# Prologue of a fused RWKV attention and soft-MoE kernel: identity copies on ScalarE, buffer clears on VectorE

## The chip, the cores and the metric

The kernel runs on one core of one Trainium2 chip. The core has five engines that the text calls by their names in the profile: PE (TensorE, matmul; PEld is its weight load), DVE (VectorE), ACT (ScalarE), POOL (GpSimd) and SP (SyncE, which issues loads). The metric is device time of one execution in microseconds (us); lower is better. Times inside an execution count from the start of the profile's span.

## The reference

The first stage is a linear attention with a decaying state, for 4 batches, 8 heads, 768 steps and head size 48. The second is a soft mixture of experts over the 3072 rows that the first one gives, with 32 slots in 8 experts.

```python
for t in range(S):                                # attention, state is D x D per batch and head
    cur = einsum('bhd,bhe->bhde', u * k[t], v[t])
    y[t] = einsum('bhd,bhde->bhe', r[t], state + cur)
    state = w * state + einsum('bhd,bhe->bhde', k[t], v[t])
...
logits = x @ phi                                  # x: 3072 x 384, phi: 384 x 32
slot_input = softmax(logits, axis=0).T @ x
slot_out = relu(slot_input[e] @ w1[e]) @ w2[e]    # per expert, 4 slots each
out = softmax(logits, axis=1) @ slot_out
```

## The kernel before

The attention is computed in chunks of 128 steps. Powers of `w` are taken up into `k` and `r` beforehand: `k` is multiplied by `w^-j` and `r` by `w^j`, with `j` the place in the chunk. The tables of these powers are `tabs` (for the short tiles, one third of the steps of a batch) and `tabl` (for the long tiles, two thirds). The attention of a chunk is then a masked matrix product, plus a product with the state.

The body of the kernel is a list of small tasks. Their order is written out by hand in the string `ORDER`; a task is put on the engine that stands behind its colon or on the first one that it allows. Each engine runs its tasks in that order. Names begin with a letter for the kind and end with the number of the tile or unit. The ones that the prediction touches are:

- `Lk0`, `Lr0`, `Lv0` and so on: loads from SP (L195).
- `Sk0`, `Sr0`, `Sk1a` and so on: the product of `k` or `r` with its table into a bf16 buffer of the tile `mix` (L423), on DVE for tile 0 and for `Sk1b`, else on POOL.
- `Tk0`, `Tr0`: transposes of such a buffer on PE (L432), with `turn` or `turnl` as the moving operand, which also sorts the steps. `Ek0`, `Er0`: the eviction (L356).
- `VC0`: the cast of `v` to bf16 on POOL (L414).
- `TB0a` and its sisters: exponentials that fill `tabl` (L393) on ACT, from arguments that DVE puts into `xT_all` (L281).
- `CB`: `consts_b`, a clear of `Mb`, two reductions of `ident_f` (L339 to L341) on DVE, and two copies on ACT (L342, L344).
- `CA` and `CU`: the transposed `w` and `u` are copied to `wuT` (DVE, L313) and multiplied into `ucol` (POOL, L316).
- `F0_3`, `F1y_9` and so on: fill matmuls that keep PE busy (L849); their results are not used.

Before these tasks stands the prologue (L209 to L304 and L330), written in plain order. POOL makes two identities, `ident` in bf16 and `ident_f` in f32, and an upper triangle `up_b`, by clears and `affine_select`. Three permuted copies of `ident` follow: `idp` (L255, DVE), which PE multiplies with `up_b` and `ident` to get the mask and the permutation `permT`; `turn` (L260, DVE, two halves); and `turnl` (L263, POOL). After the first two products PE runs thirteen warming matmuls on zeros (`keep_warm(13)`, L219). POOL clears the padding columns of the six `k` and `r` buffers in `mix` (L271), which each hold 48 columns of data in every 64, and then `ucol`, `wT`, `selp`, `nm`, `acc`, `Lc`, `uns` and one column of `x` (L296 to L331).

On DVE the prologue computes the exponents of the table (`expos_a`, L244, and `expos_b`, L247 to L249) and copies `permT` out of PSUM (L283). Then ACT takes the logarithm of `w` (L284), DVE multiplies it with the exponents into `AT_all` (L281, two halves), and ACT takes the exponentials into `tabs` (L288, L289). ACT starts with the issue of the load of `w` (L211) and a load of its function table (L212).

Of the kernel before, what the change touches and what calls it, by code (L numbers as in the profile page):

```python
# [81 lines left out]
def kernel(  # L82
# [13 lines left out]
    B, H, S, D = r.shape  # L96
# [9 lines left out]
    nQ = H // 2  # L106
    NP = B * nQ
    R = 8
    J = C // R
# [16 lines left out]
    def O(ins):  # L126
        return tc.keep_in_program_order(ins)

    pe, dve, act, pool, sp = nc.tensor, nc.vector, nc.scalar, nc.gpsimd, nc.sync
# [55 lines left out]
    Y_t = [Yb[:, j, :] for j in range(2)]  # L185
# [41 lines left out]
    ident = cst.tile([128, 128], bf, name="ident")  # L227
# [24 lines left out]
    expos_b(e17, float(JH // nQ))  # L252

    idp_t = cst.tile([128, C], bf, name="idp")
    O(dve.tensor_copy(idp_t[:].rearrange("p (j r) -> p j r", j=J), ident[:].rearrange("p (r j) -> p j r", r=R)))  # L255
    idp = idp_t[:]

    turn = cst.tile([128, 128], bf, name="turn")
    for c in range(CC):
        O(dve.tensor_copy(turn[:, 64 * c:64 * c + 64].rearrange("p (q s r) -> p q s r", q=nQ, s=2),  # L260
                          ident[:, 64 * c:64 * c + 64].rearrange("p (r s q) -> p q s r", q=nQ, s=2)))
    turnl = cst.tile([128, 128], bf, name="turnl")
    O(pool.tensor_copy(turnl[:].rearrange("p (c q r) -> p c q r", q=nQ, r=R), ident[:].rearrange("p (c r q) -> p c q r", q=nQ, r=R)))  # L263
    mask = cst.tile([128, C], f32, name="mask")
    permT = cst.tile([128, C], bf, name="permT")
# [2 lines left out]
    keep_warm(13)  # L268
    expos_a(nQ * (R - 1))
    for t in ks_t:  # L270
        O(pool.memset(t.rearrange("p (x s) -> p x s", s=64)[:, :, D:64], 0.0))  # L271

    av = AT_all[:].rearrange("p a b -> p (a b)").bitcast(f32)
    AVW = P2 * (JH + 1)
# [3 lines left out]
    def argv_part(dst, ex):  # L278
        n = ex.shape[1]
        for e in range(2):  # L280
            O(dve.tensor_mul(dst[:, e], lnw.rearrange("p (e d) -> p e d", e=2)[:, e, None, :].to_broadcast([128, n, D]),  # L281
                             ex[:, :, None].to_broadcast([128, n, D])))
    O(dve.tensor_copy(permT[:], Y_t[1][:, 0:128]))  # L283
    O(act.activation(out=lnw, in_=w_f, func=AF.Ln))  # L284
    argv_part(argv, e17[:, 0:JH + 1])
    expos_b(e17l, float(J // nQ))
# [49 lines left out]
                               phi_f[:, q, :].rearrange("p (g j s) -> p g j s", g=2, s=Spe)))  # L336

    def consts_b():
        O(dve.memset(Mb[:], 0.0))  # L339
        O(dve.tensor_reduce(out=sel[:], in_=ident_f[:].rearrange("p (b c) -> p c b", b=B), axis=AX.X, op=ALU.add))  # L340
        O(dve.tensor_reduce(out=blk[:], in_=ident_f[:].rearrange("p (b c) -> p b c", b=B), axis=AX.X, op=ALU.add))  # L341
        O(act.copy(selp[:].rearrange("p (j x) -> p j x", x=32)[:, :, 0:2 * Spe],  # L342
                   sel[:].rearrange("p (j x) -> p j x", j=EG)))
        O(act.copy(rep4[:], sel[:, None, :].to_broadcast([128, B, ES])))  # L344
# [40 lines left out]
    for j, f in enumerate((zeros_b, consts_p)):  # L385
        add(f"CB{j}", "POOL", (lambda f: lambda t: f())(f), deps=["LP"] if j else [])
    add("CB", "DVE", lambda t: consts_b())

    for h, av_, x in (("a", argl, slice(0, JH + 1)), ("b", argm, slice(JH, J + 1))):
# [578 lines left out]
```

## Time and profile before

| what | value |
|---|---|
| median of 3 runs | 124.03 us (124.11, 122.61, 124.03) |
| profiled execution, its own time | 124.79 us |
| span from first to last instruction | 123.0 us |
| busy share of the span: PE, DVE, ACT, POOL | 84%, 78%, 69%, 52% |
| mean granted TensorE clock | 0.945 |
| HBM traffic over the span | 359 GB/s |

A row of the timeline gives start, duration, engine, line, operation, output and input tiles with their shapes, and how many instructions were merged into it. In square brackets it has the time that the engine stood idle before, and what ended that. The page's second part divides the span into 40 slices with the busy share of each engine in tenths; the first six slices cover the prologue and the start of the task list. The granted clock is given per stretch as a share of full speed.

### The profile page before, as it was taken

What the parts mean: (1) busy time and instruction counts of PE and PEld (TensorE: products, weight loads), DVE (VectorE), ACT (ScalarE), POOL (GpSimd) and SP (SyncE); (2) the same over time, 40 slices, a digit from 0 to 9 for tenths busy, and PEclk for the clock granted to TensorE, in tenths of its full rate; (3) what the DMA queues carried; (4) which work ended last, traced back from release to release, by engine and by line L of the source; (5) the groups of instructions that cost most, each with busy time, mean ns of one, the idle gap of its engine ahead of it and who ended that gap; (6) DMA issues with size and microseconds to landing.
All of it is one profiled execution on the core that took longest, in us unless ns stands there. A gap on an engine that the chain in (4) does not pass through costs nothing.

```text
span 123.0 us, 4044 instructions
## 1 busy us (share of the span) xinstructions
PE 103.5 (84%) x1723; PEld 77.0 (63%) x1729; DVE 95.5 (78%) x176; ACT 84.6 (69%) x135; POOL 63.5 (52%) x85
## 2 busy tenths in 40 slices
PE   4959939999999999999999989999889979797000
PEld 1317526888888887888687877877454738573000
DVE  6989973789999999899999999999787710189000
ACT  4057569498999899999989999978744350187000
POOL 7930888899999999999999510310000000000000
PEclk9999985599999999999999999999999999999955
DMA  2999999999999899999999999999999980039994
GB/s 34 319 402 412 378 401 395 379 368 402 372 403 353 163 218 215 212 221 212 214 213 212 219 220 209 214 219 214 211 220 216 204 154 11 0 127 417 412 416 164
DMA packets 10697, 31.81 MB, mean 259 GB/s; under 512 B 1336, under 2 KB 4664, under 8 KB 10680
## 3 DMA queue, kind: packets, MB, share of 16 engines
q0 software_dynamic: 2592, 12.58, 50.4%
q1 hardware_dynamic: 7944, 18.93, 40.8%
q8 instruction: 13, 0.21, 0.7%
q10 hardware_dynamic: 144, 0.05, 0.4%
q14 instruction: 4, 0.03, 0.1%
HBM read 39.42 MB, written 4.72 MB: 359 GB/s over the span
## 4 chain that ended last, share of the span: by engine, by line
PE 51%; DVE 24%; ACT 11%; issue 4%; DMA 2%; DVEq 0%; ACTq 0%
PE T L432 9%; PE Ab L502 5%; PE T L591 4%; ACT mix L356 4%; DVE AT_all L507 4%; PE Yb L568 3%; DVE mix L935 3%; PE Yb L563 3%; PE Yb L903 3%; DVE mix L423 3%; PE T L477 2%; DVE AT_all L281 2%; PE Yb L574 2%; PE Mb L903 2%; DMA LexpT<-in_w_dram 2%
## 5 line engine op out<-in xcount | busy, mean ns | idle before, releaser
L507 DVE TENSOR_TENSOR AT_all<-Ab,mask 128x1024 bf16<-128x1024 f32 x24 | 29.1, 1214 | 1.1 <-PE Ab L502 1.1
L423 POOL TENSOR_TENSOR mix<-raw,tabl 128x768 bf16<-128x768 f32 x15 | 27.8, 1869 | 0.5 <-ACT tabl L393 0.3
L356 ACT COPY mix<-T 128x1024 bf16<-128x1024 bf16 x18 | 17.7, 1017 | 2.2 <-PE T L432 2.1
L432 PEld LDWEIGHTS <-mix 128*128 128x128 bf16 x192 | 12.1, 101 | 5.5 <-issue 2.7
L551 DVE TENSOR_TENSOR dv<-vn,Mb 128x768 bf16<-128x768 bf16 x12 | 11.3, 943 | 2.9 <-ACT wT L323 2.9
L423 POOL TENSOR_TENSOR mix<-raw,tabs 128x768 bf16<-128x768 f32 x6 | 10.9, 1825 | 0.9 <-PE T L432 0.9
L356 ACT COPY vT_all<-T 96x1024 bf16<-96x1024 bf16 x10 | 10.1, 1014 | 1.5 <-PE T L432 1.1
L356 ACT CAST x<-Yb 128x768 bf16<-128x768 f32 x12 | 9.7, 811 | 1.2 <-PE Yb L574 0.6
L502 PE MATMUL Ab<-mix 64*128 64x128 bf16 x192 | 9.8, 222 | 0.9 <-ACT mix L356 0.6
L432 PE MATMUL T<-turnl,mix 128*128 128x128 bf16 x128 | 10.1, 231 | 0.1
L356 ACT COPY xT_all<-T 128x768 bf16<-128x768 bf16 (+1 forms) x12 | 9.1, 787 | 1.4 <-PE T L591 1.3
L356 ACT COPY vn<-T 128x768 bf16<-128x768 bf16 x12 | 9.6, 811 | 0.0
L414 POOL CAST vj<-raw 128x768 bf16<-128x768 f32 x10 | 8.2, 829 | 0.9 <-DMA raw<-in_v_dram 0.9
L356 ACT COPY kn<-T 128x768 bf16<-128x768 bf16 (+1 forms) x11 | 7.8, 714 | 1.2 <-PE T L477 1.1
L448 DVE TENSOR_TENSOR pr<-T,mix 128x1024 bf16<-128x1024 bf16 x12 | 8.1, 680 | 0.1
L502 PEld LDWEIGHTS <-mix 64*128 64x128 bf16 x192 | 5.8, 95 | 3.1 <-issue 0.8
L568 PEld LDWEIGHTS <-AT_all 128*128 128x128 bf16 x192 | 6.6, 96 | 1.6
L219 PE MATMUL T<-LexpT 128*128 128x512 bf16 x15 | 6.0, 567 | 1.5 <-DVE LexpT L215 1.5
L432 PEld LDWEIGHTS <-vj 128*96 128x96 bf16 x96 | 6.7, 129 | 0.5 <-issue 0.2
L477 PE MATMUL T<-ident,mix 128*128 128x128 bf16 x80 | 6.9, 229 | 0.0
L535 DVE TENSOR_TENSOR Z<-Mb,wT 128x384 bf16<-128x384 f32 x12 | 6.6, 550 | 0.3 <-PE Mb L528 0.3
L568 PE MATMUL Yb<-vn,AT_all 128*128 128x48 bf16 x192 | 6.8, 183 | 0.0
(188 smaller groups left out, 256.1 us busy)
## 6 DMA issues: line engine op xcount, KB each, us to landing
raw<-in_moe_w_dram POOLq DMA_DIRECT2D x13, 768.0 KB, 13.3
raw<-in_k_dram SPq DMA_DIRECT2D x4, 768.0 KB, 11.4
raw<-in_r_dram SPq DMA_DIRECT2D x4, 768.0 KB, 11.7
raw<-in_v_dram SPq DMA_DIRECT2D x4, 768.0 KB, 12.1
out_dram<-mix SPq DMA_DIRECT2D x3, 768.0 KB, 4.9
raw<-in_k_dram SPq DMA_DIRECT2D x4, 384.0 KB, 9.7
raw<-in_r_dram SPq DMA_DIRECT2D x4, 384.0 KB, 9.9
raw<-in_v_dram SPq DMA_DIRECT2D x4, 384.0 KB, 10.0
```

The source lines that it names most:

```text
L356: O(act.copy(dst, src))
L414: O(act.copy(o, i_) if t.eng == "ACT" else pool.tensor_copy(o, i_))
L423: O(eng.tensor_mul(src.inst.rearrange("p (j e s) -> p e j s", j=JH, e=2)[:, :, :, 0:D], rv(), tab))
L432: O(pe.transpose(Tb.inst[0:P, jj * 128:(jj + 1) * 128], sv[:, jj, :], (turn, turnl)[lg][:]))
L448: O(dve.tensor_mul(cv(pb), tv(), cv(kT)))
L477: O(pe.transpose(Tb.inst[:, x * 128:(x + 1) * 128], kT.inst[:, x, :], ident[:]))
L502: O(pe.matmul(Abf.inst[:, e, x * C:(x + 1) * C], kT.inst[s, g * nQ + x, :], rT.inst[s, g * nQ + x, :]))
L507: O(dve.tensor_mul(AT.inst[:], Abf.inst[:].rearrange("p e (g t) -> p e g t", g=nQ), mask[:, None, None, :].to_broadcast([128, 2, nQ, C])))
L535: O(dve.tensor_mul(Smid.inst[:], Mf.inst[:, 0:SW].rearrange("p (q d) -> p q d", q=nQ)[:, :, None, :].to_broadcast([128, nQ, 2, D]), wT[:, ...
L551: O(dve.tensor_mul(dvb.inst[:].rearrange("p g e d -> p (g e) d"), vn.inst[:].rearrange("p g e d -> p (g e) d"), Mf.inst[:, 448:448 + 2 * P ...
L568: O(pe.matmul(y[:, x // nQ, q * P2 + e * D:q * P2 + (e + 1) * D], a[x // nQ].inst[:, e, q, :], vn.inst[:, x, e, :], start=False, stop=(c = ...
L903: O(pe.matmul(SO[h][32 * x:32 * x + 32, :], hT[g][:, y, 32 * x:32 * x + 32], w2_of(g * EG + x)[:, y, h * Dm // 2:(h + 1) * Dm // 2], start ...
```

## The change

Three edits in the prologue. The copies of the identity into `idp` and `turn` go from DVE to ACT, at the same place in the program; on ACT they follow the table load and precede the logarithm. The six clears of the `k` and `r` buffers go from POOL to DVE, again at the same place, which is after `expos_a` and ahead of the products into `AT_all`. And DVE's copy of `permT` out of PSUM moves from the prologue to the head of `consts_b`, that is, behind `Sk1b` in DVE's order. The copy of `turnl` and POOL's other clears stay where they are.

```diff
     idp_t = cst.tile([128, C], bf, name="idp")
-    O(dve.tensor_copy(idp_t[:].rearrange("p (j r) -> p j r", j=J), ident[:].rearrange("p (r j) -> p j r", r=R)))
+    O(act.copy(idp_t[:].rearrange("p (j r) -> p j r", j=J), ident[:].rearrange("p (r j) -> p j r", r=R)))
...
     for c in range(CC):
-        O(dve.tensor_copy(turn[:, 64 * c:64 * c + 64].rearrange("p (q s r) -> p q s r", q=nQ, s=2),
-                          ident[:, 64 * c:64 * c + 64].rearrange("p (r s q) -> p q s r", q=nQ, s=2)))
+        O(act.copy(turn[:, 64 * c:64 * c + 64].rearrange("p (q s r) -> p q s r", q=nQ, s=2),
+                   ident[:, 64 * c:64 * c + 64].rearrange("p (r s q) -> p q s r", q=nQ, s=2)))
...
     for t in ks_t:
-        O(pool.memset(t.rearrange("p (x s) -> p x s", s=64)[:, :, D:64], 0.0))
+        O(dve.memset(t.rearrange("p (x s) -> p x s", s=64)[:, :, D:64], 0.0))
...
-    O(dve.tensor_copy(permT[:], Y_t[1][:, 0:128]))
     O(act.activation(out=lnw, in_=w_f, func=AF.Ln))
...
     def consts_b():
+        O(dve.tensor_copy(permT[:], Y_t[1][:, 0:128]))
         O(dve.memset(Mb[:], 0.0))
```

## The prediction

> **What bounds the kernel now.** I read the page first (VectorE 78% busy, TensorE 84%, so no single engine is full), then the chain of waits, then the timeline of the first 24 us engine by engine, because every edited line runs there. All times below are microseconds from the start of the span. The chain of waits, with its start and length in the first two columns:
>
> ```profile
> 0.73 2.58 DMA LexpT<-in_w_dram
> 3.34 0.29 ACT LexpT L284
> 3.65 3.00 DVE AT_all L281 x2
> 6.66 0.94 ACT tabs L288 x2
> ...
> 13.52 2.14 DVE mix L423
> ...
> 16.50 0.22 ACT selp L342
> ...
> 21.59 1.06 PE T L432 x8
> ```
>
> The reader is to see that the two products of L281 take 3.00 us on the chain, although the same instruction form takes 0.59 us each when it fills `xT_all` at 10.1. The timeline of 4.6 to 5.4 us shows why they are slow (start, duration):
>
> ```profile
> 2.68 3.88 DVE L260 COPY turn<-ident 128x64 bf16<-128x64 bf16 x1
> 2.93 3.64 DVE L244 TENSOR_SCALAR pl<-pi 128x17 int32<-128x17 int32 x1
> 3.28 3.29 DVE L283 CAST permT<-Yb 128x128 bf16<-128x128 f32 x1
> 3.65 2.92 DVE L281 TENSOR_TENSOR AT_all<-LexpT,e 128x432 f32<-128x432 f32 x2
> ```
>
> Five instructions start at their normal pace and all end between 6.56 and 6.58. The second `turn` copy is the oldest of them; its twin took 0.31. GpSimd's timeline gives what stands beside them:
>
> ```profile
> 2.65 0.28 POOL L263 COPY turnl<-ident 128x128 bf16<-128x128 bf16 x1
> 2.88 1.57 POOL L271 MEMSET mix<- 128x256 bf16 x6
> ...
> 6.35 0.16 POOL L328 MEMSET x<- 128x6 bf16 x2
> 7.44 0.82 POOL L414 CAST vj<-raw 128x768 bf16<-128x768 f32 x1 [0.93 <-DMA raw<-in_v_dram]
> ```
>
> GpSimd runs clears with no gap from 2.88 to 6.51, and VectorE's five ends follow 0.05 after. I read this as one SBUF-to-SBUF copy that cannot write while GpSimd writes, and everything behind it retiring in order. TensorE's timeline and the windows (length, busy time of PE, PEld, DVE, ACT, POOL, then granted clock) matter for what comes next:
>
> ```profile
> 3.04 4.94 PE L219 MATMUL T<-LexpT 128*128 128x512 bf16 x13
> 9.22 0.61 PE L432 MATMUL T<-turn,mix 128*128 128x128 bf16 x8 [1.24 <-DVE mix L423]
> ...
> 17.67 0.37 PE L849 MATMUL T<-mix,ident 128*128 128x256 bf16 x1 [2.14 <-ACT vn L356]
> ```
>
> ```profile
> 13.85:17.26 3.41, 1.62 (x18) 0.88 (x16) 3.31 (x5) 0.91 (x4) 3.41 (x2) 1.00 1.04 385
> 17.26:20.67 3.41, 3.00 (x39) 2.05 (x39) 0.55 (x2) 3.34 (x8) 3.08 (x4) 0.50 1.04 403
> 20.67:24.09 3.42, 3.20 (x32) 2.86 (x32) 2.79 (x4) 1.89 (x2) 2.54 (x3) 0.50 1.05 378
> ```
>
> The thirteen warming products hold TensorE until 7.98 whatever VectorE does, and after a window with 1.62 us of work the granted clock is 0.50 for two windows.
>
> **The change, part by part.**
>
> *Copies on ScalarE.* ScalarE's table load lasts from 1.39 to 2.67, so `idp` cannot start before 2.67 (on VectorE it started at 2.27 and ended at 2.54). The trace has no SBUF bf16 copy of that size on ScalarE; the bounds are 0.22 (L342, 32 columns) and 0.29 (L344, 128 columns, also from SBUF). I take 0.29 for `idp` and about 0.25 for each `turn` half, their starts overlapping by about 0.1: `idp` ends at 2.96, `turn` between 3.2 and 3.5. The logarithm L284 started at 3.34, when `w` had landed, so it moves by 0 to 0.2. TensorE's L266 waited for `idp` and `up_b` and started at 2.75; now 3.05, so the warming products start at 3.34 instead of 3.04. Their starts are 0.43 apart until about 7.02 and 0.21 after it, so the later start costs half its 0.30 at the end: 8.1 instead of 7.98.
>
> *Clears on VectorE.* Six of them. VectorE's rows are 0.165 (128 words of 4 bytes, L209) and 0.27 (256 words, L215), with starts 0.14 to 0.25 apart: 0.8 to 1.5 us in all, from 2.4 to between 3.2 and 3.9. The cover is the wait for the logarithm at 3.62; the upper bound would delay L281 by 0.3, and the warming products would hide that too. On GpSimd 1.51 us goes (the first clear started at 2.88, the next line at 4.39), so its run ends at 5.0 instead of 6.5.
>
> *The stall.* With no `turn` copy on VectorE, L281 starts at 3.65 and its second half ends at 3.65 + 0.53 + 0.59 = 4.77. GpSimd's clears still run beside it until 5.0, but L249, a product of two SBUF operands, took 0.18 beside the clear of `up_b` and 0.18 with GpSimd idle, so I charge nothing. Should L244 still be caught, everything retires at 5.05; this too is hidden, by TensorE, as the next step shows. The Trainium skill, page SBUF — State Buffer, section "SBUF: two separate sides", says that the pair of ports VectorE and GpSimd share is locked for one whole instruction and the loser waits until that one finishes. By that the `turn` copy would have waited for one clear of 0.31; the trace shows 3.88, a wait through a whole row of clears, so the measurement decides.
>
> *What follows.* The `tabs` exponentials run 4.3 to 5.3 and 5.3 to 6.1. `k` has landed by then (issued 0.74, 4.1 to landing) and `r` at 5.8. Sk0 on VectorE (0.95) ends at 6.35 and Sr0 at 7.3; before, Sr0 ended at 9.95. So VectorE is 2.65 ahead. But the transposes of Sk0 now stand behind the warming products: 8.1 instead of 9.22, a gain of only 1.1. ScalarE's evictions follow and the first `tabl` exponential (L393, started 11.68, 0.86) ends at 11.4. It and the 1.9 to 2.5 earlier `wuT` release GpSimd's first product: 11.45 instead of 13.04, a gain of 1.6. VectorE's own L423 at 13.45 ran 2.21 beside GpSimd's 1.82 (alone it takes 0.95), that is, it waited its turn; now both end at 11.45 + 1.82 + 0.9 = 14.15 instead of 15.66.
>
> *The moved `permT` copy.* It now stands between that L423 and L339/L340, which release `selp`. Its own row is the stalled 3.29; bounds are 0.15 (L313, eight columns from PSUM) and 0.48 (L339, 512 columns to PSUM). I take 0.2, on the path. `selp` starts at 15.15 instead of 16.50: gain 1.35. ScalarE then works without a gap to 21.56, now 20.2.
>
> *The clock.* From 21.59 TensorE leads to VectorE's L546 at 25.16: 2.50 us of it at clock 0.50, 1.07 at full, so 2.32 us of full-speed work. TensorE's pause moves to about 14.3 to 16.2, leaving 1.5 us of work in the window 13.85:17.26, so the half clock comes again at 17.26. If it ends again at 24.09, 1.92 of the work is done by then and L546 starts at 24.5: gain 0.66. If it ends at 20.67, L546 starts at 22.8: gain 2.4. In the window 17.26:20.67 TensorE was idle for its first 0.41 us (3.00 busy, clock stayed at half); with that idle gone I count 3.2 busy, like the window that did end it. That is nearer to the upper case: I take 1.7. The Trainium skill, page TensorE: Matmul & The Clock Gate, section "Part 1: The HAM clock gate", says that these windows run freely and that the point varies from run to run; the steps of 3.41 us here agree, and their phase against the program is what I cannot know.
>
> *The rest.* From 25 to 88 us the chain is VectorE and then nearly gapless TensorE; the next loads land well ahead (`k` of the third tile at 14.4, used at 21.88), and the last weights land near 102.2 and are used after 106. Nothing there takes the gain back, and I add nothing.
>
> Sum: profiled execution 124.79 (span 123.0 and 1.8 around it) minus 1.7 gives 123.1. The median of the runs, 124.03, is 0.76 below the profiled one, so the forecast is 122.3.
>
> **The rivals.**
>
> *No half clock at all.* For it: the pause is only 1.9 us in a 3.41 window, and the window 7.02:10.43 kept the clock with 1.91 us of work. Against it: my count leaves 1.5. It would give 1.35 + 1.25 (half of the 2.50) = 2.6: 121.4, and below it if the 2.65 of VectorE carries.
>
> *The stall is not GpSimd's doing.* Then VectorE stays held and only costs remain: 0.1 at the warming products and 0.2 for `permT`. Time 124.3. Against it: five equal ends at 0.05 behind GpSimd's last.
>
> *Slower: the clock comes late.* TensorE got full speed at 7.02, one window after 3.61. Busy from 3.04 it had 0.57 to spare, from 3.34 it has 0.27. If a boundary falls into the 0.30 lost, full speed comes at 10.43 or, with a window not filled, at 13.85. The thirteen products then end at 9.1, and the 0.95 + 3.37 us of TensorE work up to 13.85 runs at half speed: 4.3 later, of which the pause of 2.14 takes at most 2.1. I take 2.7: 126.7. For it: `idp` does wait behind the table load. Against it: 0.30 in 3.41 is 9%.
>
> **How the numbers follow.** Forecast 0.58, no half clock 0.20, stall elsewhere 0.09, late clock 0.13. What a measurement of this kernel can tell from no change is about 2%, that is 121.55 and 126.51. The forecast case spans gains of 0.66 to 2.4, and the runs differ by 1.5 us among themselves, so 0.26 of its chance lies beyond 2%. Faster: 0.26 + 0.20 = 0.46. Within: 0.32 + 0.09 = 0.41. Slower: 0.13. The range runs from 120.3 (the second rival's 121.4 less the spread of runs) to 125.3 (the upper run, with the costs and part of a late clock); it leaves out the late clock and little else.
>
> **What would show it.** Right: L281 ends near 4.8, Sr0 near 7.3, the warming products still end near 8.1 and the transposes follow at once, GpSimd's first L423 starts near 11.4 and `selp` near 15.2. Wrong: VectorE instructions that again end together behind GpSimd; transposes at 9 or later; a granted clock of 0.50 where it now is 1.00.

## The result and the profile after

| | kernel before | changed kernel |
|---|---|---|
| median of 21 runs each | 123.95 us (122.61 to 126.24) | 124.26 us (123.63 to 126.03) |
| ratio, with its 95% interval | | 1.0056 [1.0029, 1.0084] |
| profiled execution, its own time; span | 124.79; 123.0 us | 125.18; 123.4 us |
| mean granted TensorE clock in it | 0.945 | 0.961 |

The change made the kernel slower, by a quarter to half a per cent; the forecast had been 1.4% faster. That is a small move, and the clock of the profiled execution is higher than before, so the loss has to be found in the order of the work.

The 108 runs of the kernel before fall into two groups with none between: 27 from 121.27 to 122.87 us and 81 from 123.31 to 126.87. Where the granted clock is on record (87 runs), its median is 0.957 in both, so the clock does not divide them; what does was not measured, and no run of the smaller group left a profile. The ratio in the table leaves out the runs that are more than 1.5% above the fastest of their kernel (the medians of all 21 give 1.0025 [1.0012, 1.0062]), and in most of the later comparisons that limit lies in the gap and would keep the smaller group alone, so all further comparisons are ratios of the medians of all runs, with a 95% interval from resampling the runs. The times are told apart to about half a per cent in this way. A gain against the kernel before is a gain against its larger group.

The front of the kernel did what the change is for. The next lines are from the timeline of the changed kernel (start, duration, engine, line), engine by engine:

```profile
2.41 0.87 DVE L271 MEMSET mix<- 128x128 uint32 x6
3.73 1.13 DVE L281 TENSOR_TENSOR AT_all<-LexpT,e 128x432 f32<-128x432 f32 x2 [0.45 <-ACT LexpT L283]
5.45 1.83 DVE L423 TENSOR_TENSOR mix<-raw,tabs 128x768 bf16<-128x768 f32 x2
...
2.68 0.42 ACT L255 COPY idp<-ident 128x128 bf16<-128x128 bf16 x1
...
4.78 0.16 POOL L327 MEMSET x<- 128x6 bf16 x2
7.46 2.81 POOL L414 CAST vj<-raw 128x768 bf16<-128x768 f32 x1 [2.52 <-DMA raw<-in_v_dram]
...
3.45 5.17 PE L219 MATMUL T<-LexpT 128*128 128x512 bf16 x13
8.46 1.06 PE L432 MATMUL T<-turn,mix 128*128 128x128 bf16 x16
```

The reader is to see that L281 no longer runs for 3 us and ends at 4.86, that the two products of L423 end at 7.28 where they had ended at 9.95, and that TensorE's transposes follow the warming products at 8.46 in place of 9.22. The warming products end later than before (8.62, before 7.98), but the tasks on this path are ahead up to here. GpSimd's cast of L414 is not: it takes 2.81 us in place of 0.82 and ends at 10.27, before at 8.26.

Then TensorE stands still. These are the rows of the same timeline around 14 us, of VectorE, TensorE and ScalarE; the bracket gives the idle time ahead of a row and what ended it:

```profile
12.54 1.99 DVE L423 TENSOR_TENSOR mix<-raw,tabl 128x768 bf16<-128x768 f32 x1 [0.19 <-ACT tabl L393]
14.45 0.28 DVE L338 CAST permT<-Yb 128x128 bf16<-128x128 f32 x1
14.84 0.48 DVE L339 MEMSET Mb<- 128x512 f32 x1
...
14.79 0.59 PE L849 MATMUL Yb<-mix,ident 128*128 128x512 bf16 x1 [3.21 <-DVE permT L338]
15.59 1.27 PE L849 MATMUL Yb<-mix,ident 128*128 128x512 bf16 x3 [0.22 <-issue]
16.66 0.84 PE L487 MATMUL T<-ident,vT_all 96*128 96x96 bf16 x8
...
15.57 0.22 ACT L342 COPY selp<-sel 128x32 f32<-128x32 f32 x1 [2.33 <-DVE sel L340]
...
17.54 0.80 ACT L356 COPY vn<-T 128x768 bf16<-128x768 bf16 x1 [1.55 <-PE T L487]
```

In the kernel before, the same tasks stood at these times:

```profile
12.50 1.15 PE L849 MATMUL Yb<-mix,ident 128*128 128x512 bf16 x4
13.58 0.51 PE L487 MATMUL T<-ident,vT_all 96*128 96x96 bf16 x8
...
16.83 0.79 ACT L356 COPY vn<-T 128x768 bf16<-128x768 bf16 x1
```

The fill task `F1y_9`, whose results nobody reads, used to start at 12.50. It writes the tile `Yb`. The copy into `permT` reads the other half of that tile, and it now stands behind `Sk1b` in VectorE's order, so the fill waits 3.21 us until 14.79. Behind it in TensorE's order stands `V0` (L487), whose eviction `vn` ScalarE could have taken up at 15.9, behind its two copies from `sel`. Instead `vn` starts at 17.54; in the kernel before it was 16.83. The windows (length, busy time of PE, PEld, DVE, ACT, POOL, then the granted clock) show a second cost of the pause, in the same execution:

```profile
10.43:13.85 3.42, 1.14 (x23) 0.98 (x21) 2.60 (x3) 2.81 (x4) 2.15 (x3) 1.00 0.99 359
13.85:17.26 3.41, 2.25 (x12) 1.29 (x13) 2.84 (x6) 0.42 (x2) 3.12 (x2) 0.63 1.06 402
17.26:20.67 3.41, 3.41 (x54) 2.25 (x52) 0.00 (x0) 3.06 (x7) 1.51 (x1) 0.87 1.03 402
```

The half clock begins at 14.72, just ahead of `F1y_9` and `V0`, and ends at 18.14: the late work also runs at half pace (L487 takes 0.84 where it took 0.51). The kernel before had two windows at half clock in its profile, so L546 still comes earlier than there (24.69, before 25.16); but that profile is not the typical execution, as will be seen. The changed kernel's profiled execution also lost its 0.47 again later, in steps near 46, 58 to 62 and 71 us. What makes the steps was not sought, and nothing is built on them. A second profile of the same kernel, from another run, has a span of 122.5 and no such steps. It shows the same wait (2.69 us ahead of `F1y_9`) and the half clock over it (13.11 to 19.94). Its `vn` starts at 16.75, 0.08 ahead of before, so that hardly anything is left of the lead.

### The profile page after: what moved, and what is told of

Read it like the earlier page. It is cut to its first block, busy times and chain, and to the rows that moved or that the text cites. A ratio compares the mean times of both kernels' runs of the same rounds, so it can differ in the third digit from the quotient of the medians.

```text
span 123.4 us, 4042 instructions
## 1 busy us (share of the span) xinstructions
PE 102.5 (83%) x1723; PEld 75.8 (61%) x1729; DVE 93.2 (76%) x179; ACT 85.8 (70%) x138; POOL 63.8 (52%) x79
## 4 chain that ended last, share of the span: by engine, by line
PE 58%; DVE 17%; POOL 8%; issue 6%; ACT 2%; DVEq 0%; POOLq 0%
PE T L432 10%; POOL mix L423 5%; PE Ab L502 5%; PE T L219 4%; DVE AT_all L507 4%; PE Yb L568 4%; PE T L591 3%; PE Yb L563 3%; DVE mix L935 3%; PE Yb L574 3%; PE Yb L903 3%; PE T L477 2%; PE T L487 2%; PE Mb L903 2%; PE Mb L528 2%
## 5 line engine op out<-in xcount | busy, mean ns | idle before, releaser
L423 POOL TENSOR_TENSOR mix<-raw,tabl 128x768 bf16<-128x768 f32 x15 | 27.7, 1864 | 3.4 <-ACT tabl L393 2.2
L432 PEld LDWEIGHTS <-mix 128*128 128x128 bf16 x192 | 11.4, 98 | 0.9
L414 POOL CAST vj<-raw 128x768 bf16<-128x768 f32 x10 | 10.1, 1021 | 2.5 <-DMA raw<-in_v_dram 2.5
L423 POOL TENSOR_TENSOR mix<-raw,tabs 128x768 bf16<-128x768 f32 x6 | 10.9, 1818 | 0.0
L432 PE MATMUL T<-turnl,mix 128*128 128x128 bf16 x128 | 9.3, 219 | 0.0
L849 PEld LDWEIGHTS <-ident 128*128 128x128 bf16 x37 | 3.5, 109 | 6.6 <-issue 5.8
L487 PE MATMUL T<-ident,vT_all 96*128 96x96 bf16 x96 | 6.6, 212 | 0.6 <-issue 0.4
## 6 DMA issues: line engine op xcount, KB each, us to landing
raw<-in_v_dram SPq DMA_DIRECT2D x4, 384.0 KB, 10.2
```

What stands on the lines that cost most here:

```text
L414: O(act.copy(o, i_) if t.eng == "ACT" else pool.tensor_copy(o, i_))
L423: O(eng.tensor_mul(src.inst.rearrange("p (j e s) -> p e j s", j=JH, e=2)[:, :, :, 0:D], rv(), tab))
L432: O(pe.transpose(Tb.inst[0:P, jj * 128:(jj + 1) * 128], sv[:, jj, :], (turn, turnl)[lg][:]))
L487: O(pe.transpose(Tb.inst[:, x * P2:(x + 1) * P2], vT.inst[:, x, :], ident[0:P2, 0:P2]))
```

## The experiments

The theory after this reading: the stall was worth about 1 us, and the moved `permT` copy costs more than that, by the wait of `F1y_9` on the tile. The rivals: the later warming products and the later full clock cost it (from the copies on ScalarE); or VectorE itself loses what it gains, by the clears it took over; or the pause's half clock decides, whatever makes the pause.

**The copy's source moved to another tile.** The changed kernel, with the product behind `permT` in the bank `Mb`, which no fill task writes that early. The copy stays late.

```diff
-    O(pe.matmul(Y_t[1][:, 0:128], idp, ident[:], start=True, stop=True))
+    O(pe.matmul(Mb[:, 0:128], idp, ident[:], start=True, stop=True))
...
-        O(dve.tensor_copy(permT[:], Y_t[1][:, 0:128]))
+        O(dve.tensor_copy(permT[:], Mb[:, 0:128]))
```

> The changed kernel, but the product that permT is copied from is written to the PSUM tile Mb and read from there; F1y_9 then shares no tile with that copy. Theory W (the new wait of F1y_9 for the moved permT copy ate the gain): F1y_9 starts near 11.6 instead of 14.79, the eviction VE0 near 15.9 instead of 17.54 (before: 16.83), and the time is 0.5 to 1.5 us below the kernel before, 122.5 to 123.4. Theory C (the stall's removal is worth nothing on the path, and the later start of the warming products, the clock and scatter make the loss): VE0 may come earlier, but the time stays at 124.0 to 124.5, a ratio of 1.000 to 1.008.

Measured: 122.90 us, 0.9922 [0.989, 0.997] of the kernel before. TensorE's and ScalarE's timeline:

```profile
11.43 1.15 PE L849 MATMUL Yb<-mix,ident 128*128 128x512 bf16 x5
...
15.90 0.79 ACT L356 COPY vn<-T 128x768 bf16<-128x768 bf16 x1
```

`F1y_9` starts 3.4 us earlier, `vn` follows `selp` at once, and the kernel is now faster than the one before (by the means of all runs the ratio is 0.9954 [0.992, 1.000]). The copy at its late place, with its 0.28 us in VectorE's chain, is thus cheap; the wait on the tile is what cost. The half clock is there in this profile too (0.60 on average from 17.26 to 20.67 us), so it does not decide by itself.

**The move of the `permT` copy alone**, on the kernel before:

```diff
-    O(dve.tensor_copy(permT[:], Y_t[1][:, 0:128]))
     O(act.activation(out=lnw, in_=w_f, func=AF.Ln))
...
     def consts_b():
+        O(dve.tensor_copy(permT[:], Y_t[1][:, 0:128]))
```

> The kernel before with the one edit that moves the permT copy to the head of consts_b. Theory W: PE stands idle from about 12.6 to 16.0 ahead of F1y_9, VE0 comes near 18.5 instead of 16.83, and the time is 0.7 to 2 us above before, 124.7 to 126. Theory C: no more than 0.2 us above before, since only a copy of 0.2 us is added to VectorE's chain.

Measured, in six runs: 125.34 us, 1.0119 [1.0045, 1.0198]. The same wait is there without the rest of the change:

```profile
16.04 1.32 PE L849 MATMUL Yb<-mix,ident 128*128 128x512 bf16 x5 [3.35 <-DVE permT L338]
...
18.04 0.80 ACT L356 COPY vn<-T 128x768 bf16<-128x768 bf16 x1 [0.80 <-PE T L487]
```

Here `F1y_9` starts 0.8 us ahead of the half clock (0.50 from 16.84 to 20.25), and `vn` still comes 1.21 later than before.

**The copies on ScalarE alone**, and **the clears on VectorE alone**, each on the kernel before:

```diff
-    O(dve.tensor_copy(idp_t[:].rearrange("p (j r) -> p j r", j=J), ident[:].rearrange("p (r j) -> p j r", r=R)))
+    O(act.copy(idp_t[:].rearrange("p (j r) -> p j r", j=J), ident[:].rearrange("p (r j) -> p j r", r=R)))
...
-        O(dve.tensor_copy(turn[:, 64 * c:64 * c + 64].rearrange("p (q s r) -> p q s r", q=nQ, s=2),
+        O(act.copy(turn[:, 64 * c:64 * c + 64].rearrange("p (q s r) -> p q s r", q=nQ, s=2),
...
```

> The kernel before with idp and turn copied on ScalarE and nothing else changed. If VectorE's stall comes from the turn copy caught by GpSimd's clears, L281 ends near 4.9 although GpSimd clears until 6.5, Sr0 ends near 7.4 and the transposes of tile 0 start near 8.5, behind the warming products. Theory W: no wait at F1y_9, time 0.5 to 1.5 us below before. Theory C: same as before or up to 0.5 us above it. If the stall is not the copy's doing, L281 still ends at 6.5.

```diff
-        O(pool.memset(t.rearrange("p (x s) -> p x s", s=64)[:, :, D:64], 0.0))
+        O(dve.memset(t.rearrange("p (x s) -> p x s", s=64)[:, :, D:64], 0.0))
```

> The kernel before with the six clears on VectorE and nothing else changed. The turn copy stays on VectorE, so it should be caught until GpSimd's shorter run of clears ends at 5.0, with everything behind it ending together at 5.05. The warming products keep their start at 3.04 and end near 8.0, so the transposes of tile 0 start near 8.1, earlier than in the changed kernel (8.46). Theory W: time 0.5 to 1.7 us below before, at least as good as with the copies alone. Theory C: same as before.

Measured: 123.21 us, 0.9948 [0.992, 0.997], and 123.23 us, 0.9949 [0.989, 0.999]. Each gains about 0.65 us by itself. By the means of all runs the gains are about half that (0.9972 and 0.9970) and their intervals reach 1, so that each gains is less sure than that neither loses. Neither the copies nor the clears are the cost, and the two rivals that put it there fall. The timelines held two things that were not foreseen. With the copies gone from VectorE, a smaller victim was caught in the profile of the first, the cast of L247, until GpSimd's last clear ended at 6.48, and Sr0 ended at 9.30 where 7.4 had been expected; the next lines are VectorE's and GpSimd's:

```profile
4.96 1.55 DVE L247 CAST pf<-pl 128x17 f32<-128x17 int32 x1
...
6.32 0.16 POOL L328 MEMSET x<- 128x6 bf16 x2
```

And with the clears gone from GpSimd, the second `turn` copy ran beside GpSimd's other clears without being caught, where a hold until about 5.05 had been expected:

```profile
2.71 0.53 DVE L260 COPY turn<-ident 128x64 bf16<-128x64 bf16 x2
...
2.88 0.18 POOL L296 MEMSET ucol<- 128x8 bf16 x1
```

**The change again, and the change with the `permT` copy at its old place.** The first is the changed kernel unaltered, so that it stands beside the second on the same chip; the second's edit against it is the diff of the `permT` copy above, backwards.

> The changed kernel once more, on one chip with the three others and the kernel before. Theory W (the wait of F1y_9 for permT): 0.3 to 0.7 us above before and 1.0 to 1.6 us above the kernel with the copies and clears alone; F1y_9 again released by the permT copy near 14.8. If the first result was scatter, it comes out level with before.

> The changed kernel with the permT copy back at its old place in the prologue: copies on ScalarE and clears on VectorE, nothing else. Theory W: F1y_9 starts near 11.6 behind A00, VE0 near 15.6 to 15.9, time 0.5 to 1.2 us below before. Theory C (stall's removal worth nothing, other costs): level with the changed kernel.

Measured: 124.32 us, 1.0048 [1.0004, 1.0083], and 122.71 us, 0.9918 [0.986, 0.997]. Between the two lies a ratio of 1.0131 [1.0081, 1.0183], that is 1.6 us for the one moved line. Copies and clears together gain 1.0 us (0.9931 [0.989, 0.998] by the means). `F1y_9` and `vn` stand where they were expected:

```profile
11.39 1.15 PE L849 MATMUL Yb<-mix,ident 128*128 128x512 bf16 x4
...
15.45 0.79 ACT L356 COPY vn<-T 128x768 bf16<-128x768 bf16 x1
```

The gain is against the larger group of runs of the kernel before. Against the median of its smaller group, 122.42, neither the 122.71 nor the median of any other version told of here is a gain. The 1.6 us between the two versions do not hang on these groups.

**Fewer warming products**, on the clears alone:

```diff
-    keep_warm(13)
+    keep_warm(9)
```

> The clears on VectorE alone, and nine warming products instead of thirteen. If the warming products are the next bound, as predicted, the transposes of tile 0 start near 7.0 instead of 7.94 and the whole moves by 0.5 to 0.9 us against the clears alone (to 122.3 to 122.7). If the next bound is VectorE's wuT copy, which releases GpSimd's first table product, the transposes come earlier but that product stays near 11.4 and the time moves by less than 0.3. If the full clock comes a window later for want of work, it is 0.5 us or more slower than the clears alone.

Measured: 123.11 us, 0.9991 [0.996, 1.007] of the clears alone: no difference. The transposes start at 7.98 here as against 7.94, now released by VectorE's product and not by the warming. What the profile shows besides is worth more: in this execution the `turn` copy was caught, with the same VectorE and GpSimd prologue in which it had slipped through before. From its timeline:

```profile
2.45 2.59 DVE L260 COPY turn<-ident 128x64 bf16<-128x64 bf16 x2
2.93 2.13 DVE L244 TENSOR_SCALAR pl<-pi 128x17 int32<-128x17 int32 x1
...
4.83 0.16 POOL L328 MEMSET x<- 128x6 bf16 x2
```

Both VectorE rows end within 0.07 of GpSimd's 4.99, as the five had in the kernel before. So whether a copy is caught is settled by small shifts in time. The six profiles with the `turn` copies on VectorE show which: in four (the kernel before, the `permT` move alone, nine products, and the fill alone, told of next) L249 starts at 2.18 and the first `turn` copy at 2.45, and the second copy is caught; in two (the clears alone, and the clears with the fill) L248 takes 0.44 in place of 0.29, L249 starts at 2.32 to 2.33 and the copies at 2.70 to 2.71, and none is caught. That this also divides the runs of the kernel before into their two groups would fit, but is not shown.

The nine products have a cost of their own in this profile: TensorE works 1.78 us in 7.22 to 10.64, and the clock is 0.50 from 10.64 to 14.05, a window that the clears alone have at 1.00. With the copy caught and the clock halved, this run does not tell what the four products are worth.

**TensorE's pause filled.** Seven more fill products of 512 columns (not used; the 14 in `F2by_14` counts 256 columns each) behind the transposes `Tk1a`, just ahead of the pause before `vn`; tried on the clears alone, on copies and clears together, and on the kernel before.

```diff
-Lv1 Ev0 TB1b Sk1b:DVE Lk2 CB A00 F1y_9 V0 Lr2 F2_7 Tk1a Sr1b VC1a VE0:ACT TB1a F3_1 Tk1b NE0:ACT F4y_4 U0 CW Lv2
+Lv1 Ev0 TB1b Sk1b:DVE Lk2 CB A00 F1y_9 V0 Lr2 F2_7 Tk1a F2by_14 Sr1b VC1a VE0:ACT TB1a F3_1 Tk1b NE0:ACT F4y_4 U0 CW Lv2
```

> The clears on VectorE alone, and a fill task of seven more matmuls into the Y bank behind Tk1a, in TensorE's pause ahead of VE0 (13.9 to 16.0 with the clears alone). The products are computed and not used. If the half clock from 17.4 to 20.8 comes of that pause, it goes away, PE's work there runs at full speed, and the time falls by 0.3 to 1.0 us against the clears alone, with less scatter from run to run. If the half clock costs nothing on the path, the time stays within 0.2.

> The copies on ScalarE and the clears on VectorE, the permT copy at its old place in the prologue, and one more task of fill products (F2by_14, its products are not used) behind Tk1a in TensorE's order. Theory A (the wait of F1y_9 was all that cost, and filling TensorE's pause ahead of vn keeps full clock): F1y starts near 11.4, VE0 (vn) near 15.4, no window at 0.50 or 0.63 between 10 and 30 us, and the lead over the kernel before at 25 us stays to the end; median of all runs 1.0 to 1.8 us below the kernel before (ratio 0.985 to 0.992). Theory B (the half clock is hidden by other waits, filling gains nothing): the half clock is gone, and the ratio is that of the same kernel without the fill, 0.992 plus or minus 0.003. A ratio over 0.995 would say that the extra fills themselves delay the tasks behind them.

> The kernel before with one thing added: fill products F2by_14 (not used) behind Tk1a in TensorE's order; the prologue is unchanged, VectorE's stall to 6.56 stays. Theory A (the half clock costs what the prediction worked out, up to 2.5 us in the kernel before's profile): the two windows at 0.50 from 17.26 to 24.09 are gone, L546 starts near 23 where it started at 25.16, and the ratio of medians is 0.982 to 0.992. Theory B (at half clock TensorE is behind others only part of the time, and most runs of the kernel before have one window or none): the ratio is 0.994 to 1.002, and the prologue's stall is worth as much with the fill as without it.

Measured: 122.57 us with the clears, 0.9947 [0.991, 1.004] of the clears without the fill; 122.41 us with copies and clears, 0.9891 [0.986, 0.994] of the kernel before and 0.9976 [0.992, 1.0045] of the same without the fill; 123.61 us for the fill alone, 0.9988 [0.997, 1.002] of the kernel before. The third is the plainest. Its windows from 10.2 us on have no half clock left:

```profile
10.20:13.60 3.40, 3.40 (x45) 2.30 (x42) 3.40 (x8) 3.40 (x5) 1.13 (x3) 1.00 1.02 377
13.60:17.00 3.40, 3.22 (x27) 1.61 (x25) 3.29 (x5) 0.89 (x4) 3.40 (x2) 1.00 1.06 397
17.00:20.40 3.40, 2.50 (x44) 1.70 (x44) 1.26 (x2) 3.33 (x8) 3.05 (x4) 1.00 1.03 398
```

The page's row of the granted clock in 40 slices of that kernel is full until the last two:

```profile
PEclk9999999999999999999999999999999999999955
```

L546, at 25.16 in the profile of before, came at 23.82. Yet the median did not move. The theory that the clock is worth up to 2.5 us gets no support; the other, that at half clock TensorE is behind others only part of the time and most executions have one such window or none, fits. A cost of the added products themselves, which would hide a gain from the clock, is not excluded. The stall in front is worth as much with full clock: copies and clears with the fill are 0.9903 [0.987, 0.995] of the fill alone, 1.2 us.

## Why the prediction was wrong

*The step that failed is "The moved `permT` copy".* It named what stands behind the copy on VectorE (`L339`, `L340`, `selp`) and charged 0.2 us there. The copy took 0.28, so that term was right in size. What it left out is who waits for the copy's input to be read: a writer of the same PSUM tile on another engine, and all that stands behind that writer in TensorE's order. The rows for it were there: `F1y_9` wrote `Yb` at 12.50, and the last read of `permT` from `Yb` ended at 6.57, so the order between them held with 5.9 us to spare. Moved behind `Sk1b`, which the prediction itself put at 14.15, the copy ends at 14.4. Then come `F1y_9` and `V0`, 1.59 together in the profile of before, and `vn` at 16.0: 0.8 ahead of before, where the forecast would have had 15.5. At half clock, which a pause of this length had brought in the profile of before, the two take twice as long and `vn` comes at 17.6, 0.8 behind before; measured was 17.54. With the source in another tile the kernel went to 0.9922, with the copy at its old place to 0.9918, and with the move alone to 1.0119: the three runs show it.

*Copies on ScalarE.* The sign was right, a size was off: `idp` took 0.42 instead of 0.29, so L266 started at 3.16 and not 3.05 and the warming products at 3.45 and not 3.34. They ended at 8.62 (forecast 8.1), as the full clock came at 7.90 (two windows of 3.41 ahead of the half clock at 14.72) instead of 7.02, and the lead of the transposes fell to 0.76 from the forecast 1.1. Most of that lateness goes with the execution and not with the copies: in the second profile of the same kernel the products start at 3.46 and end at 7.83, and in four profiles of other versions with the copies on ScalarE they start at 3.46 to 3.48 and end at 7.92 to 8.79. The whole window that the "late clock" rival had foreseen was lost in none of them.

*Clears on VectorE* took 0.87 (forecast 0.8 to 1.5), and *the stall* was GpSimd's doing: L281 ended at 4.86 (forecast 4.77), and with the clears still on GpSimd the cast of L247 was held to their end. *What follows* held to 0.5: Sr0 ended at 7.28 (7.3), GpSimd's first L423 came at 11.90 (11.45), `selp` at 15.57 (15.15). With the `permT` copy back at its old place `selp` starts at 15.12.

*The clock* turned the 1.35 us at `selp` into 0.66 to 2.4 at L546, and it was mis-sized apart from the step that failed. It was read from one execution with two windows at 0.50 and a mean clock of 0.945. Of the 87 runs of the kernel before that were taken beside the experiments, 11 had a mean clock under 0.95 (median span 123.2 us), 46 lay between 0.95 and 0.965 (122.05), and 30 above (121.8). One window at half clock is 0.014 of this mean. In the larger of the two groups of runs alone the three medians are 123.2, 122.3 and 121.9, so there a second window goes with 0.9 us and a first with 0.4. That two windows are dear was right, but most executions have no second one to gain back. The gain that is there, 1.0 us for copies and clears, comes without the clock, since it is 1.2 us in the medians where neither kernel's profile has a half clock between 10 and 30 us.

The changed kernel is another matter: none of its 33 runs had a mean clock over 0.965, and its span follows the clock more closely (correlation -0.87, interval -0.97 to -0.64; before -0.36, -0.53 to -0.16). This fits a pause that always costs a window, with late work in it. At the same clock, between 0.95 and 0.965, its median span is 122.4, against 122.05 for all runs of the kernel before and 122.3 for its larger group. How much of the loss is the half clock, and how much the late work, was not measured.

The Trainium skill, page "TensorE: Matmul & The Clock Gate", section "Part 1: The HAM clock gate", says that the windows run freely against the program. The spread of the clock over these 87 runs agrees; it is a reason to take a clock term from several executions and not from one.

*The rest* held, but for the steps in the one profile told of above: the lead that TensorE has early on is kept (for copies and clears with the fill against the fill alone, 0.87 us at 10.7 us and 0.83 at 48; `selp` at 15.55 and 16.35; spans 121.1 and 121.9).

Of the tell-tales, "Right" came out nearly whole while the time went the other way. They watched the steps that had been costed, and none watched TensorE's order between 11 and 16 us. One sign of "Wrong" did come, a granted clock of 0.50 from 14.72, where it had been 1.00 up to 17.26. In the range, the 121.4 that is called the second rival's is that of "No half clock at all", the first in the list.

## What to carry to other kernels

When a read is moved later, look for the next writer of its tile on every engine, in each engine's own order, and price all that stands behind that writer: the trace of before shows it as an order that is kept with time to spare, not as a wait (5.9 us here). Fill work that only keeps TensorE warm should write to a tile that no one reads late. A clock term belongs to many executions, not to the profiled one. Of the versions run here, copies and clears with the `permT` copy left in the prologue are the one to take (0.9918 [0.986, 0.997]); with the pause filled the median is lower still (0.9891), though the two cannot be told apart.

## What the runs showed of the hardware

- One small VectorE copy or cast between SBUF tiles beside a gapless row of GpSimd clears was held until the whole row had ended, and VectorE instructions behind it that had started at their pace ended with it: 3.88 us before, 2.4 us in the run with nine warming products, 1.55 us for the cast of L247. A `turn` copy that started 0.25 us later was not held; there a GpSimd clear of eight columns took 0.18 where it else took 0.10, so GpSimd seems to have waited.
- GpSimd's cast of L414 took 2.81 us beside VectorE's unbroken two-operand products, and 0.82 in the kernel before. In the second profile of the changed kernel it took 2.71, and TensorE's transposes of its output waited 0.33 for it.
- ScalarE's copy of 128 bf16 columns in a strided order took 0.42 us; the estimate from a copy of 128 columns of another kind had been 0.29.
- A window of 3.41 us with 1.91 us of TensorE work was followed by full clock (7.02 to 10.43 in the kernel before), one with 1.78 by half (7.22 to 10.64 with nine products).
